# A decode step of attention and MLP: accumulator rows as products of 512 columns, and the other 64 columns of up to eight rows in one product

## The chip, the cores and the metric

The kernel runs on one core of one Trainium2 chip. The metric is the time of one execution on the device, in microseconds; the number given for a kernel is the median of several executions. A profile of one execution stands beside it.

## The reference, cut to what matters

The kernel computes one step of decoding for two sequences: attention against a cache of 4096 keys and values with 32 heads, a two-layer MLP with GELU, and a gate that mixes both. All data are float32.

```python
B, Sq, D = 2, 1, 576;  H, Sk, Dh = 32, 4096, 128;  F = 4608
x = A_x
g = sigmoid((x * gate_w).sum(-1, keepdims=True))
# attention over the cache
q = (x @ wq).reshape(B, Sq, H, Dh).transpose(0, 2, 1, 3)
p = softmax(einsum("bhqd,bhkd->bhqk", q, k_cache) * Dh ** -0.5, axis=-1)
o = einsum("bhqk,bhkd->bhqd", p, v_cache)
a = o.transpose(0, 2, 1, 3).reshape(B, Sq, H * Dh) @ wo        # wo: 4096 x 576
# MLP
b = gelu(x @ w1 + b1, approximate=True) @ w2 + b2              # w2: 4608 x 576
return g * a + (1 - g) * b
```

## The kernel before, in words

**Tiles.** The caches are read in 16 steps (`N`), each with the keys or values of four heads of one sequence (8 MB). In SBUF there is one large tile, `ring`, of three slots; each K, each V and, at the end, each of three groups of rows of w2 and wo (`LAST`) takes the next slot. At the start wq and w1 lie in the same tile, and what is needed for a short time only (`temp`) lies behind them in the third slot. `load()` issues the next transfer of the list `seq` on the queue of SyncE (SP); `load_next` says that a slot's content is used up and issues what may now go there. The last group goes into the slot of the last V.

**A step.** VectorE (DVE) multiplies the K tile by q (L483), GpSimd (POOL) and DVE add up along the head's dimension (L487 to L489), DVE takes the maximum (L493), TensorE (PE) spreads it (L498), ScalarE (ACT) takes the exponential (L508), and TensorE multiplies V by the weights (`av`, L519): 32 products of 512 columns. A product has 32 columns of weights at most, and four of them go to the four groups of 32 output partitions in turn. `keep` (L531) and `combine` (L537) put the step's result into `oall`.

**The output rows.** The second half of the MLP and the output projection are sums of products of one row each: row r of w2 (36 rows, of 128 partitions each), the part `wx` (the last row of w2, split up), and row r of wo (32 rows). Each row has 576 columns. `acc_mm` (L355) adds such a row into the accumulator `acc` in PSUM: two products of 288 columns with two columns of weights each (for the two sequences), at partitions 64 * (r % 2) + 32 * s for the halves s. So `acc` holds four partial sums of 288 columns. It starts with b2 times 1 - g. `mlp_out` does rows of w2, `mlp_x` the part `wx`, `wo_out` rows of wo.

**The order at the end** is written by hand: behind the last scores `mlp_out(0, 24)`, then the last V's `av`, `keep` and `combine`, then `norm_sum`, `norm_t` and `o_turn` (the scaled result of the attention is transposed into `oP`), with further rows of w2 between them, then `mlp_x` and `wo_out(0, FOLD)` with FOLD = 23. `last_out` copies `acc` to SBUF (L438), multiplies wo's rows 23 to 31 into `res` (L441: four products of 144 columns a row, at four groups of partitions), adds the four partial sums of `acc` by products with `fold` behind row 26 (L452), copies `res` and writes the output (L464). wo's rows arrive in pieces, the last ones in pieces of one row and less, so that each is multiplied as it lands.

**At the start** there are products of x with wq and w1 (L291), a first accumulating product of b2 (L355 with g1z), the GELU on DVE and ACT, which gives `hg`, and `hx` for the part `wx` (L397 to L407).

Of the kernel before, what the change touches and what calls it, by code (L numbers as in the profile page):

```python
# [8 lines left out]
F32 = mybir.dt.float32  # L9
AF = mybir.ActivationFunctionType  # L10
ALU = mybir.AluOpType
AX = mybir.AxisListType
P = 128
# [6 lines left out]
def kernel(  # L20
# [14 lines left out]
    nc = tc.nc  # L35
    B, H, SK, DH = k_cache.shape
    D = x.shape[-1]
# [21 lines left out]
    NC = 4  # L59
    DO = D // NC  # L60
    NS = 2
    DS = D // NS
    SCALE = float(DH) ** -0.5
    SLOTS = 3

    LAST = (
        (("w2", 0, 14), ("w2", 14, 28)),
        (("w2", 28, 35), ("wx", 0, 4), ("wo", 0, 9), ("wo", 9, 17)),
        (("wo", 17, 23), ("wo", 23, 27), ("wo", 27, 30), ("wo", 30, 31), ("wo", 31, 32)),
    )  # L70
    FOLD = 23
    SLOT = R * DH
# [8 lines left out]
    cp = ctx.enter_context(tc.tile_pool(name="cp", bufs=1))  # L81
# [4 lines left out]
    ps_acc = ctx.enter_context(tc.tile_pool(name="ps_acc", bufs=1, space=bass.MemoryType.PSUM))  # L86
    ps_av = ctx.enter_context(tc.tile_pool(name="ps_av", bufs=2, space=bass.MemoryType.PSUM))
    ps_big = ctx.enter_context(tc.tile_pool(name="ps_big", bufs=1, space=bass.MemoryType.PSUM))
    ps_o = ctx.enter_context(tc.tile_pool(name="ps_o", bufs=1, space=bass.MemoryType.PSUM))
# [6 lines left out]


    ring = rp.tile([P, SLOTS * SLOT], F32, name="ring")
    kt, vt, wqt, w1t, rows = {}, {}, {}, {}, {}
    seq = [(w, c) for w in ("wq", "w1") for c in range(len(ROWS[w]) + 1)]  # L100
    for i in range(N):
        seq += [("k", i), ("v", i)]
# [19 lines left out]
    def slot(n):  # L122
        k = len(held) % SLOTS
        return ring[:, k * SLOT:k * SLOT + n]
# [8 lines left out]
    NR = NF - 1  # L133
# [3 lines left out]
    def load_last(m):  # L137
        n = sum(z - a for _, a, z in LAST[m]) * D

        used["e"], used["z"] = len(held) % SLOTS * SLOT + n, (len(held) % SLOTS + 1) * SLOT  # L140
        t = slot(n)
        o = 0
        for w, a, z in LAST[m]:
            if w == "wx":
                x2 = t[:32, o:o + z * D]
                rows[w] = x2
                o += z * D
                for c in range(4):
                    nc.sync.dma_start(x2[c::4].rearrange("e (s n) -> e s n", s=4), srcx2[c])
                continue  # L150

            ends = (a * D, a * D + DS, a * D + DS + DO, z * D) if (w, z) == ("wo", 32) else (a * D, z * D)
            for u, v in zip(ends, ends[1:]):
                nc.sync.dma_start(t[:, o:o + v - u], srcs[w][:, u:v])
                o += v - u
            for r in range(a, z):
                rows[w, r] = t[:, o - (z - r) * D:o - (z - r - 1) * D]

    def temp(n, parts=P):
        t = ring[:parts, used["t"]:used["t"] + n]  # L160
        used["t"] += n
        assert used["t"] <= SLOTS * SLOT
        return t

    def late(n, parts=P):
        t = ring[:parts, used["e"]:used["e"] + n]
        used["e"] += n
        assert not seq and used["e"] <= used["z"]
# [28 lines left out]
    b2r = temp(D, 1)  # L197
# [17 lines left out]
    ident = cp.tile([P, P], F32, name="ident")  # L215
# [3 lines left out]
    idsc = cp.tile([P, P], F32, name="idsc")  # L219
    nc.vector.tensor_scalar_mul(idsc, ident, SCALE)  # L220

# [4 lines left out]
    NO = N * E  # L226
    pt = []
    for j in range(NPB):
        t = cp.tile([P, NT * EB + 32 - EB], F32, name=f"p{j}")
# [39 lines left out]
    g1 = cp.tile([P, B], F32, name="g1")  # L269
# [76 lines left out]

    acc = ps_acc.tile([P, DS], F32, name="acc")

    def acc_mm(lhsT, rhs, k, start=False, stop=False):
        m = lhsT.shape[-1]
        for s in range(NS):
            o = 64 * (k % 2) + 32 * s
            nc.tensor.matmul(  # L355
                acc[o:o + m], lhsT, rhs[:, s * DS:(s + 1) * DS], start=start, stop=stop, skip_group_check=True
            )

    g1z = cp.tile([1, 2, 32], F32, name="g1z")
    nc.vector.memset(g1z, 0.0)  # L360
    nc.vector.tensor_copy(g1z[:, 0, :B], g1[0:1])
    for k in range(2):
        acc_mm(g1z[:, k], b2r, k, start=True)

    fold = cp.tile([P, NS, B], F32, name="fold")
    nc.vector.tensor_add(
        fold, ident[:, :P // 2].rearrange("p (s c) -> p s c", s=NS)[:, :, :B],
        ident[:, P // 2:].rearrange("p (s c) -> p s c", s=NS)[:, :, :B],
    )


    hps = [ps_av.tile([P, 512], F32, tag="av", name=f"hps{m}") for m in range(FB - 1)]
# [12 lines left out]
    hg = cp.tile([P, NF, B], F32, name="hg")  # L385
    t = temp(NF * B).rearrange("p (r b) -> p r b", b=B)
# [4 lines left out]
    nc.vector.tensor_scalar(t, t, 1.0, 0.5, op0=ALU.add, op1=ALU.mult)  # L391
    nc.vector.tensor_mul(t, t, hb)
    nc.vector.tensor_mul(hg, t, g1.unsqueeze(1).to_broadcast([P, NF, B]))
    load()

    mod4 = cp.tile([P, 4], F32, name="mod4")
    nc.vector.tensor_reduce(mod4, ident.rearrange("p (q s) -> p s q", s=4), AX.X, ALU.add)  # L397
    div4 = cp.tile([P, 32], F32, name="div4")
    nc.vector.tensor_reduce(div4, ident.rearrange("p (q s) -> p q s", s=4), AX.X, ALU.add)
    hm = cp.tile([P, 4, B], F32, name="hm")  # L400
    nc.vector.tensor_mul(
        hm, hg[:, NR:].to_broadcast([P, 4, B]), mod4.unsqueeze(2).to_broadcast([P, 4, B])
    )
# [2 lines left out]
    hx = cp.tile([32, 4, B], F32, name="hx")  # L406
    nc.vector.tensor_copy(hx.rearrange("p s b -> p (s b)"), hxps)  # L407

    def mlp_x():
        for s in range(4):  # L410
            acc_mm(hx[:, s], rows["wx"][:, s * D:(s + 1) * D], s)

    def mlp_out(lo, hi):
        for r in range(lo, hi):
            acc_mm(hg[:, r], rows["w2", r], r)

    KB = DH // 32
    oP = cp.tile([P, B, 32], F32, name="oP")  # L420

    def o_turn(turn):
        t = late(B * 32).rearrange("p (b c) -> p b c", c=32)
        for b in range(B):
            nc.vector.transpose(t[:, b], oT[:, b])
        ps = ps_sm.tile([P, B * 32], F32, tag="sm", name="op_t")
        nc.tensor.matmul(ps, turn, t.rearrange("p b c -> p (b c)"), start=True, stop=True)
        nc.vector.tensor_copy(oP.rearrange("p b c -> p (b c)"), ps)

    def wo_out(lo, hi):  # L430
        for r in range(lo, hi):
            acc_mm(oP[:, :, r], rows["wo", r], r)


    def last_out():
        res = ps_big.tile([32 * (NC - 1) + B, DO], F32, tag="big", name="res")
        sums = late(DS)
        nc.scalar.copy(sums, acc)  # L438

        def part(r, s):  # L440
            nc.tensor.matmul(  # L441
                res[32 * s:32 * s + B], oP[:, :, r], rows["wo", r][:, s * DO:(s + 1) * DO],
                start=r == FOLD, stop=r == 31, skip_group_check=True,
            )

        for r in range(FOLD, 31):
            for s in range(NC):
                part(r, s)
            if r == FOLD + 3:
                for s in range(NC):  # L450
                    h, o = divmod(s * DO, DS)
                    nc.tensor.matmul(  # L452
                        res[32 * s:32 * s + B], fold[:, h], sums[:, o:o + DO],
                        start=False, stop=False, skip_group_check=True,
                    )

        osb = late(D, B)
        for h in ((0, 1), (2,), (3,)):
            for s in h:
                part(31, s)  # L460
            for s in h:
                cpy = nc.vector.tensor_copy if s % 2 == 0 else nc.scalar.copy
                cpy(osb[:, s * DO:(s + 1) * DO], res[32 * s:32 * s + B])  # L463
        nc.sync.dma_start(out.rearrange("b s d -> (b s) d"), osb)  # L464
# [2 lines left out]
    st, mx, mt, bias, avs = {}, {}, {}, {}, {}  # L467
    oT = cp.tile([P, B, H], F32, name="oT")

    oall = ps_o.tile([NO, 512], F32, name="oall")  # L470
    gall = cp.tile([NO, 1], F32, name="gall")
    gsel = cp.tile([NO, B], F32, name="gsel")
    nc.vector.tensor_reduce(
# [30 lines left out]
    def softmax(i):  # L504
        p = pt[i % NPB][:, :NT * EB].rearrange("p (t c) -> p t c", c=EB)
        for e in range(E):
            w = slice(e * PE_, (e + 1) * PE_)
            nc.scalar.activation(  # L508
                p[w, :, e * RB:(e + 1) * RB], st[i][w].rearrange("p (t c) -> p t c", c=RB), AF.Exp,
                bias=bias[i][w, e:e + 1], scale=SCALE, accum_out=rs[w, i * E + e:i * E + e + 1],  # L510
            )
# [47 lines left out]
    for i in range(N):  # L559
        k = i - 1  # L560
# [18 lines left out]
    k = N - 1  # L579
    max_n(k)  # L580
    softmax(k)
    mlp_out(0, 24)
    av(k)
    load_next(("v", k))
    assert not seq
# [3 lines left out]
    nc.vector.tensor_copy(turn.rearrange("p (h k) -> p k h", k=KB), ident.rearrange("p (k h) -> p k h", k=KB))  # L589
    osum = late(DH, NO)  # L590
    norm_sum()
    mlp_out(24, 30)
    norm_t()
    mlp_out(30, 33)
    o_turn(turn)
    mlp_out(33, NR)
    mlp_x()
    wo_out(0, FOLD)
    last_out()
# [28 lines left out]
```

## Time and profile before

| | |
|---|---|
| median of 3 runs | 723.1 us (721.8 to 723.15) |
| the profiled execution | 723.16 us |
| its span, first to last instruction | 721.0 us |
| busy: DVE, PE, POOL, ACT | 518.4, 237.9, 143.2, 37.8 us |
| DMA queue of SP | 308.55 MB, 99.0% of 16 engines |
| mean rate | 428 GB/s over the span |

A product of float32 shows as two MATMUL records in the profile, so xcounts of TensorE are twice the number of products in the code. In a row of the timeline stand the start, the length, engine and line, the operation, and what ended the idle time before it. PEld are the weight loads of TensorE. The granted clock is the share of TensorE's full clock.

### The profile page before, as it was taken

The numbers are of one execution on the slowest core, as the hardware profiler recorded it, in microseconds if no ns is written. First come the engines' busy times: TensorE is split into PE (matmuls) and PEld (weight loads), VectorE is DVE, ScalarE is ACT, GpSimd is POOL, SyncE is SP. The second block draws the span as 40 slices with busy tenths as digits, with TensorE's granted clock in tenths as the row PEclk, the third lists the DMA queues.
The fourth block names the chain that finished last, engine by engine and source line by source line (L and its number), as shares of the span: only waits on it lengthen the run. The fifth ranks groups of instructions, "written<-read, shape, count | busy, mean of one in ns | idle before, by whom it ended". The sixth has DMA issues, their size and how long they took to land.

```text
span 721.0 us, 3934 instructions
## 1 busy us (share of the span) xinstructions
PE 237.9 (33%) x1675; PEld 72.7 (10%) x1675; DVE 518.4 (72%) x154; ACT 37.8 (5%) x141; POOL 143.2 (20%) x28
## 2 busy tenths in 40 slices
PE   0754022240416060604142230506060603123197
PEld 0321000010101010101010000101010101000032
DVE  0004969889696969696969789696969596978810
ACT  0010010100001010101010100001010101010000
POOL 1000130404050404021130404040504012040400
PEclk9977557575757575655757575757575665757599
DMA  9999999999999999999999999999999999999996
GB/s 408 411 449 423 436 436 419 451 419 451 422 451 423 444 429 440 419 436 429 437 433 433 440 434 433 440 429 444 425 440 425 426 436 433 436 436 434 418 429 277
DMA packets 7261, 308.84 MB, mean 428 GB/s; under 512 B 830, under 2 KB 1214, under 8 KB 1612
## 3 DMA queue, kind: packets, MB, share of 16 engines
q1 hardware_dynamic: 7220, 308.55, 99.0%
q8 instruction: 13, 0.21, 0.1%
q10 hardware_dynamic: 24, 0.05, 0.0%
q14 instruction: 4, 0.03, 0.0%
HBM read 308.59 MB, written 0.00 MB: 428 GB/s over the span
## 4 chain that ended last, share of the span: by engine, by line
DMA 46%; DVE 35%; PE 17%; ACT 1%; issue 1%; POOL 0%; ACTq 0%; DVEq 0%; SPq 0%; POOLq 0%
DMA ring<-in_A_k_cache_dram 39%; DVE ring L483 19%; DVE s L488 10%; PE av L519 9%; DVE s L489 5%; DMA ring<-in_A_wo_dram 3%; DMA ring<-in_gate_w_dram 3%; PE hps L291 2%; PE qps L291 1%; PE oall L537 1%; PE acc L355 1%; PE mt L498 1%; DMA ring<-in_B_b_dram 1%; ACT p L508 1%; PE qps L316 0%
## 5 line engine op out<-in xcount | busy, mean ns | idle before, releaser
L483 DVE TENSOR_TENSOR ring<-ring,q 128x16384 f32<-128x16384 f32 x16 | 275.6, 17225 | 103.7 <-DMA ring<-in_A_k_cache_dram 103.7
L487 POOL TENSOR_TENSOR ring<-ring 128x3968 f32<-128x3968 f32 x16 | 137.0, 8564 | 488.7 <-DVE ring L483 488.7
L488 DVE TENSOR_REDUCE s<-ring 128x66 f32<-128x8448 f32 x16 | 143.3, 8953 | 1.3
L519 PE MATMUL av<-ring,p 128*32 128x512 f32 x1024 | 136.8, 694 | 11.4 <-ACT p L508 6.1
L498 PE MATMUL mt<-idsc,m 128*128 128x128 f32 x32 | 12.7, 500 | 359.8 <-DVE m L493 359.8
L489 DVE TENSOR_REDUCE s<-ring 128x62 f32<-128x3968 f32 x16 | 68.4, 4276 | 0.0
L508 ACT ACTIVATE p<-s,bs 32x128 f32<-32x128 f32 x64 | 25.5, 398 | 485.4 <-DVE bs L502 484.2
L519 PEld LDWEIGHTS av<-ring,p 128*32 128x32 f32 x1024 | 36.1, 126 | 121.8 <-issue 105.1
L498 PEld LDWEIGHTS mt<-idsc,m 128*128 128x128 f32 x32 | 8.0, 313 | 375.5 <-DVE m L493 314.2
L537 PE MATMUL oall<-avs,pick 128*64 128x512 f32 x32 | 30.6, 1059 | 0.8 <-DVE avs L531 0.8
L339 PE MATMUL qb<-qm,spread 64*128 64x512 f32 x8 | 7.3, 1014 | 70.4 <-POOL qm L335 70.4
L531 DVE TENSOR_TENSOR avs<-av,selr 128x512 f32<-128x512 f32 x16 | 10.9, 682 | 16.3 <-PE av L519 16.3
L249 DVE COPY ring<-ring 3x64 f32<-3x64 f32 x2 | 0.3, 182 | 19.1 <-DMA ring<-in_gate_w_dram 19.1
L378 DVE TENSOR_TENSOR ring<-hps,ring 128x384 f32<-128x384 f32 x3 | 1.7, 559 | 15.9 <-PE hps L291 15.7
L335 POOL TENSOR_TENSOR qm<-qall,mine 64x512 f32<-64x512 f32 x4 | 4.1, 1032 | 44.7 <-ACT qall L318 44.7
L310 DVE COPY ring<-ident 128x8 f32<-128x8 f32 x8 | 0.7, 169 | 15.5 <-DMA ring<-in_B_b_dram 15.5
L508 ACT ACTIVATION_READ_ACCUMULATOR p<-s,bs 32x1 f32 x64 | 11.8, 184 | 0.0
L291 PE MATMUL hps<-ring 128*32 128x384 f32 x120 | 11.5, 549 | 0.0
L355 PE MATMUL acc<-ring,hg 128*2 128x288 f32 x140 | 11.3, 467 | 0.0
L291 PE MATMUL qps<-ring 128*32 128x512 f32 x80 | 10.2, 668 | 0.0
L463 DVE COPY ring<-res 2x144 f32<-2x144 f32 x2 | 0.6, 300 | 13.1 <-PE res L441 13.0
L339 PEld LDWEIGHTS qb<-qm,spread 64*128 64x128 f32 x8 | 1.8, 279 | 73.4 <-POOL qm L335 73.4
(88 smaller groups left out, 76.3 us busy)
## 6 DMA issues: line engine op xcount, KB each, us to landing
ring<-in_B_w_dram SPq DMA_DIRECT2D x2, 4608.0 KB
ring<-in_B_w_dram SPq DMA_DIRECT2D x2, 4032.0 KB
ring<-in_A_wo_dram SPq DMA_DIRECT2D x1, 2592.0 KB
ring<-in_A_wo_dram SPq DMA_DIRECT2D x1, 2304.0 KB
ring<-in_B_w_dram SPq DMA_DIRECT2D x1, 2016.0 KB, 12.7
ring<-in_A_wo_dram SPq DMA_DIRECT2D x1, 1728.0 KB
ring<-in_B_w_dram SPq DMA_DIRECT2D x1, 1152.0 KB
ring<-in_A_wo_dram SPq DMA_DIRECT2D x1, 1152.0 KB, 19.0
```

The lines of the kernel that those rows point to most:

```text
L291: nc.tensor.matmul(ps[32 * j:32 * j + 32, :width], lhs, ts[c][:, o:o + width], start=(k == 0), stop=last, skip_group_check=True,)
L339: nc.tensor.matmul(ps, spread, t.rearrange("p u d -> p (u d)"), start=True, stop=True)
L355: nc.tensor.matmul(acc[o:o + m], lhsT, rhs[:, s * DS:(s + 1) * DS], start=start, stop=stop, skip_group_check=True)
L483: nc.vector.tensor_mul(kt[i], kt[i], qs[i].unsqueeze(1).to_broadcast([P, R, DH]))
L487: nc.gpsimd.tensor_add(t[:, :, :DH2], t[:, :, :DH2], t[:, :, DH2:])
L488: nc.vector.tensor_reduce(st[i][:, HALVED:], kt[i][:, HALVED:], AX.X, ALU.add)
L489: nc.vector.tensor_reduce(st[i][:, :HALVED], t[:, :, :DH2], AX.X, ALU.add)
L498: nc.tensor.matmul(mt[i], mx[i].to_broadcast([P, P]), idsc, start=True, stop=True)
L508: nc.scalar.activation(p[w, :, e * RB:(e + 1) * RB], st[i][w].rearrange("p (t c) -> p t c", c=RB), AF.Exp, bias=bias[i][w, e:e + 1], scale ...
L519: nc.tensor.matmul(ps[32 * j:32 * j + 32], p[:, EB * t:EB * t + 32], vt[i][:, RB * t:RB * (t + 1)].rearrange("p r d -> p (r d)"), start=(t ...
L531: nc.vector.tensor_mul(t, avs[i].rearrange("p (r d) -> p r d", d=DH), selr.unsqueeze(2).to_broadcast([P, RB, DH]))
L537: nc.tensor.matmul(oall, pick[:, NO - E - i * E:2 * NO - E - i * E], avs[i].rearrange("p r d -> p (r d)"), start=(i == 0), stop=(i == N - ...
```

## The change

- `acc` gets 512 columns. A row's first 512 columns are one product, at partitions 32 * (r % 4). So `acc` holds four partial sums of 512 columns.
- The other 64 columns of up to eight neighbouring rows are one product (`rest_mm`): its weights are the two columns of each of the rows (up to 16), its moving operand the last 64 columns of each (up to 512), and it goes to a second accumulator, `part_r`, at partitions from 0 on. Of its result only the blocks on the diagonal are wanted. These products stand behind rows 7, 13, 21, 27 and 34 of w2, behind the part `wx`, and behind rows 7, 15 and 22 of wo.
- `last_out` takes the blocks of the diagonal out of `part_r` on DVE (a multiplication by `ownr` and a sum over the blocks) and adds them with one product with `foldr`, behind the products with `fold`.
- Ahead of the last V's `av` stand rows 0 to 13 of w2 in place of 0 to 23; the others stand behind it.
- Row 16 of wo moves from the second group of `LAST` to the third, and the pieces end at rows 8 and 16.
- `res` moves to the PSUM bank of `oall`; `part_r` has the one that `res` had. Some small tiles move from the pool of constants into the third slot, and one `load()` therefore stands behind `hx`.

```diff
+    DM = 512
+    DR = D - DM
+    NB = DM // DR
...
-        (("w2", 28, 35), ("wx", 0, 4), ("wo", 0, 9), ("wo", 9, 17)),
-        (("wo", 17, 23), ("wo", 23, 27), ("wo", 27, 30), ("wo", 30, 31), ("wo", 31, 32)),
+        (("w2", 28, 35), ("wx", 0, 4), ("wo", 0, 8), ("wo", 8, 16)),
+        (("wo", 16, 23), ("wo", 23, 27), ("wo", 27, 30), ("wo", 30, 31), ("wo", 31, 32)),
...
-    acc = ps_acc.tile([P, DS], F32, name="acc")
-
-    def acc_mm(lhsT, rhs, k, start=False, stop=False):
+    acc = ps_acc.tile([P, DM], F32, name="acc")
+
+    def acc_mm(lhsT, rhs, k, start=False):
         m = lhsT.shape[-1]
-        for s in range(NS):
-            o = 64 * (k % 2) + 32 * s
-            nc.tensor.matmul(
-                acc[o:o + m], lhsT, rhs[:, s * DS:(s + 1) * DS], start=start, stop=stop, skip_group_check=True
-            )
+        o = 32 * (k % 4)
+        nc.tensor.matmul(acc[o:o + m], lhsT, rhs[:, :DM], start=start, stop=False, skip_group_check=True)
...
-    for k in range(2):
-        acc_mm(g1z[:, k], b2r, k, start=True)
+    for k in range(4):
+        acc_mm(g1z[:, min(k, 1)], b2r, k, start=True)
+    b2t = cp.tile([1, DR], F32, name="b2t")
+    nc.vector.tensor_copy(b2t, b2r[:, DM:])
...
+    def rest_mm(lhsT, rhs, n):
+        start = not part_r
+        if start:
+            part_r.append(ps_big.tile([NB * B, DM], F32, tag="big", name="acc_r"))
+            assert n == NB
+        nc.tensor.matmul(
+            part_r[0][:n * B, :n * DR], lhsT, rhs[:, :, DM:], start=start, stop=False, skip_group_check=True
+        )
+        if start:
+            nc.tensor.matmul(
+                part_r[0][:B, :DR], g1[0:1], b2t, start=False, stop=False, skip_group_check=True
+            )
...
     def mlp_out(lo, hi):
         for r in range(lo, hi):
             acc_mm(hg[:, r], rows["w2", r], r)
+            for a, z in ((0, 8), (8, 14), (14, 22), (22, 28), (28, 35)):
+                if r == z - 1:
+                    g = a - a % 14
+                    rest_mm(
+                        hg[:, a:z].rearrange("p r b -> p (r b)"), runs["w2", g][:, a - g:z - g], z - a
+                    )
...
     def wo_out(lo, hi):
         for r in range(lo, hi):
-            acc_mm(oP[:, :, r], rows["wo", r], r)
+            acc_mm(oP[:, r], rows["wo", r], r)
+            for a, z in ((0, 8), (8, 16), (16, FOLD)):
+                if r == z - 1:
+                    rest_mm(oP[:, a:z].rearrange("p r b -> p (r b)"), runs["wo", a], z - a)
...
     def last_out():
-        res = ps_big.tile([32 * (NC - 1) + B, DO], F32, tag="big", name="res")
-        sums = late(DS)
+        res = ps_o.tile([32 * (NC - 1) + B, DO], F32, tag="o", name="res")
+        sums = late(DM)
         nc.scalar.copy(sums, acc)
+        own = late(DM, NB * B).rearrange("p (r n) -> p r n", n=DR)
+        nc.vector.tensor_mul(
+            own, part_r[0].rearrange("p (r n) -> p r n", n=DR), ownr.unsqueeze(2).to_broadcast([NB * B, NB, DR])
+        )
+        tail = late(DR, NB * B)
+        nc.vector.tensor_reduce(tail, own.rearrange("p r n -> p n r"), AX.X, ALU.add)
...
-                    h, o = divmod(s * DO, DS)
+                    n = min(DO, DM - s * DO)
                     nc.tensor.matmul(
-                        res[32 * s:32 * s + B], fold[:, h], sums[:, o:o + DO],
+                        res[32 * s:32 * s + B, :n], fold, sums[:, s * DO:s * DO + n],
                         start=False, stop=False, skip_group_check=True,
                     )
+                nc.tensor.matmul(
+                    res[32 * s:32 * s + B, n:], foldr, tail, start=False, stop=False, skip_group_check=True,
+                )
...
-    mlp_out(0, 24)
+    mlp_out(0, 14)
     av(k)
...
-    mlp_out(24, 30)
+    mlp_out(14, 20)
     norm_t()
-    mlp_out(30, 33)
+    mlp_out(20, 24)
     o_turn(turn)
-    mlp_out(33, NR)
+    mlp_out(24, NR)
     mlp_x()
     wo_out(0, FOLD)
     last_out()
```

More of the change, by code (lines that the diff above doesn't have):

```diff
@@ L98 @@
     ring = rp.tile([P, SLOTS * SLOT], F32, name="ring")
-    kt, vt, wqt, w1t, rows = {}, {}, {}, {}, {}
+    kt, vt, wqt, w1t, rows, runs = {}, {}, {}, {}, {}, {}
     seq = [(w, c) for w in ("wq", "w1") for c in range(len(ROWS[w]) + 1)]
@@ L145, in load_last @@
                 x2 = t[:32, o:o + z * D]
-                rows[w] = x2
+                runs[w, 0] = x2.rearrange("p (r n) -> p r n", n=D)
                 o += z * D
@@ L155, in load_last @@
                 o += v - u
+            runs[w, a] = t[:, o - (z - a) * D:o].rearrange("p (r n) -> p r n", n=D)
             for r in range(a, z):
@@ L345 @@
     q_unit(0)
-    acc = ps_acc.tile([P, DS], F32, name="acc")
-    def acc_mm(lhsT, rhs, k, start=False, stop=False):
+    acc = ps_acc.tile([P, DM], F32, name="acc")
+    def acc_mm(lhsT, rhs, k, start=False):
         m = lhsT.shape[-1]
-        for s in range(NS):
-            o = 64 * (k % 2) + 32 * s
-            nc.tensor.matmul(
-                acc[o:o + m], lhsT, rhs[:, s * DS:(s + 1) * DS], start=start, stop=stop, skip_group_check=True
-            )
-    g1z = cp.tile([1, 2, 32], F32, name="g1z")
+        o = 32 * (k % 4)
+        nc.tensor.matmul(acc[o:o + m], lhsT, rhs[:, :DM], start=start, stop=False, skip_group_check=True)
+    g1z = temp(64, 1).rearrange("p (k c) -> p k c", k=2)
     nc.vector.memset(g1z, 0.0)
     nc.vector.tensor_copy(g1z[:, 0, :B], g1[0:1])
-    for k in range(2):
-        acc_mm(g1z[:, k], b2r, k, start=True)
[L365 to L368, printed above, removed]
-    )
+    for k in range(4):
+        acc_mm(g1z[:, min(k, 1)], b2r, k, start=True)
+    b2t = cp.tile([1, DR], F32, name="b2t")
+    nc.vector.tensor_copy(b2t, b2r[:, DM:])
+    fold = cp.tile([P, B], F32, name="fold")
+    nc.vector.tensor_reduce(
+        fold, ident.rearrange("p (g c) -> p c g", g=4)[:, :B], AX.X, ALU.add
+    )
+    foldr = cp.tile([NB * B, B], F32, name="foldr")
+    nc.vector.tensor_reduce(
+        foldr, ident[:NB * B, :NB * B].rearrange("p (r b) -> p b r", b=B), AX.X, ALU.add
+    )
+    ownr = cp.tile([NB * B, NB], F32, name="ownr")
+    nc.vector.tensor_reduce(
+        ownr, ident[:NB * B, :NB * B].rearrange("p (r b) -> p r b", b=B), AX.X, ALU.add
+    )
+    part_r = []
+    def rest_mm(lhsT, rhs, n):
[10 more added lines that the diff above has]
+            )
     hps = [ps_av.tile([P, 512], F32, tag="av", name=f"hps{m}") for m in range(FB - 1)]
@@ L393 @@
     nc.vector.tensor_mul(hg, t, g1.unsqueeze(1).to_broadcast([P, NF, B]))
-    load()
-    mod4 = cp.tile([P, 4], F32, name="mod4")
+    mod4 = temp(4)
     nc.vector.tensor_reduce(mod4, ident.rearrange("p (q s) -> p s q", s=4), AX.X, ALU.add)
-    div4 = cp.tile([P, 32], F32, name="div4")
+    div4 = temp(32)
     nc.vector.tensor_reduce(div4, ident.rearrange("p (q s) -> p q s", s=4), AX.X, ALU.add)
-    hm = cp.tile([P, 4, B], F32, name="hm")
+    hm = temp(4 * B).rearrange("p (s b) -> p s b", b=B)
     nc.vector.tensor_mul(
@@ L407 @@
     nc.vector.tensor_copy(hx.rearrange("p s b -> p (s b)"), hxps)
+    load()
     def mlp_x():
         for s in range(4):
-            acc_mm(hx[:, s], rows["wx"][:, s * D:(s + 1) * D], s)
+            acc_mm(hx[:, s], runs["wx", 0][:, s], s)
+        rest_mm(hx.rearrange("p s b -> p (s b)"), runs["wx", 0], 4)
     def mlp_out(lo, hi):
@@ L415, in mlp_out @@
             acc_mm(hg[:, r], rows["w2", r], r)
+            for a, z in ((0, 8), (8, 14), (14, 22), (22, 28), (28, 35)):
[4 more added lines that the diff above has]
+                    )
     KB = DH // 32
-    oP = cp.tile([P, B, 32], F32, name="oP")
+    oP = cp.tile([P, 32, B], F32, name="oP")
     def o_turn(turn):
@@ L427, in o_turn @@
         nc.tensor.matmul(ps, turn, t.rearrange("p b c -> p (b c)"), start=True, stop=True)
-        nc.vector.tensor_copy(oP.rearrange("p b c -> p (b c)"), ps)
+        nc.vector.tensor_copy(oP, ps.rearrange("p (b c) -> p c b", b=B))
     def wo_out(lo, hi):
         for r in range(lo, hi):
-            acc_mm(oP[:, :, r], rows["wo", r], r)
+            acc_mm(oP[:, r], rows["wo", r], r)
+            for a, z in ((0, 8), (8, 16), (16, FOLD)):
+                if r == z - 1:
+                    rest_mm(oP[:, a:z].rearrange("p r b -> p (r b)"), runs["wo", a], z - a)
     def last_out():
-        res = ps_big.tile([32 * (NC - 1) + B, DO], F32, tag="big", name="res")
-        sums = late(DS)
+        res = ps_o.tile([32 * (NC - 1) + B, DO], F32, tag="o", name="res")
+        sums = late(DM)
         nc.scalar.copy(sums, acc)
+        own = late(DM, NB * B).rearrange("p (r n) -> p r n", n=DR)
+        nc.vector.tensor_mul(
+            own, part_r[0].rearrange("p (r n) -> p r n", n=DR), ownr.unsqueeze(2).to_broadcast([NB * B, NB, DR])
+        )
+        tail = late(DR, NB * B)
+        nc.vector.tensor_reduce(tail, own.rearrange("p r n -> p n r"), AX.X, ALU.add)
         def part(r, s):
             nc.tensor.matmul(
-                res[32 * s:32 * s + B], oP[:, :, r], rows["wo", r][:, s * DO:(s + 1) * DO],
+                res[32 * s:32 * s + B], oP[:, r], rows["wo", r][:, s * DO:(s + 1) * DO],
                 start=r == FOLD, stop=r == 31, skip_group_check=True,
@@ L450, in last_out @@
                 for s in range(NC):
-                    h, o = divmod(s * DO, DS)
+                    n = min(DO, DM - s * DO)
                     nc.tensor.matmul(
-                        res[32 * s:32 * s + B], fold[:, h], sums[:, o:o + DO],
+                        res[32 * s:32 * s + B, :n], fold, sums[:, s * DO:s * DO + n],
                         start=False, stop=False, skip_group_check=True,
                     )
+                nc.tensor.matmul(
+                    res[32 * s:32 * s + B, n:], foldr, tail, start=False, stop=False, skip_group_check=True,
+                )
         osb = late(D, B)
@@ L468 @@
     oT = cp.tile([P, B, H], F32, name="oT")
-    oall = ps_o.tile([NO, 512], F32, name="oall")
+    oall = ps_o.tile([NO, 512], F32, tag="o", name="oall")
     gall = cp.tile([NO, 1], F32, name="gall")
```

## The prediction

> **What bounds the kernel now.** I read the page first (span and the two DMA rows), then the chain of waits for the last 80 us, then the timeline of TensorE alone for the last 40 us, then the busy time by stretch.
>
> ```profile
> span 721.0 us, 3934 instructions
> ...
> DMA  9999999999999999999999999999999999999996
> ```
>
> The 16 DMA engines are over 90% busy in every slice but the last. Nothing in the first 680 us can be made shorter by other products: what can move is the end, where the last rows of wo land and are multiplied. The chain of waits there (start, length, what):
>
> ```profile
> 692.58 3.49 PE av L519 x32
> 696.07 20.26 DMA ring<-in_A_wo_dram
> ...
> 716.37 1.97 PE res L441 x40
> ...
> 718.36 0.27 ACT ring L463
> ```
>
> The last transfers are issued when the last V's products have freed their slot, land at 716.3 us, and then come the products of wo's last rows and a copy. The timeline of TensorE shows how it meets these landings (start, length, what, idle time before it):
>
> ```profile
> 682.10 0.80 PE L498 MATMUL mt<-idsc,m 128*128 128x128 f32 x2 [26.15 <-DVE m L493]
> ...
> 684.72 7.86 PE L355 MATMUL acc<-ring,hg 128*2 128x288 f32 x96
> 692.41 7.04 PE L519 MATMUL av<-ring,p 128*32 128x512 f32 x64
> ...
> 700.27 1.07 PE L537 MATMUL oall<-avs,pick 128*64 128x512 f32 x2 [0.82 <-DVE avs L531]
> ...
> 702.90 0.27 PE L554 MATMUL oT_t<-ident,ring 64*128 64x64 f32 x1
> 703.10 1.14 PE L355 MATMUL acc<-ring,hg 128*2 128x288 f32 x12
> 704.17 0.43 PE L427 MATMUL op_t<-ring 128*128 128x64 f32 x2
> 704.54 0.67 PE L355 MATMUL acc<-ring,hg 128*2 128x288 f32 x8
> 705.13 1.15 PE L355 MATMUL acc<-ring,hx 32*2 32x288 f32 x16
> 706.21 4.53 PE L355 MATMUL acc<-ring,oP 128*2 128x288 f32 x68
> 711.55 1.64 PE L355 MATMUL acc<-ring,oP 128*2 128x288 f32 x24 [0.80 <-DMA ring<-in_A_wo_dram]
> 714.29 1.17 PE L441 MATMUL res<-ring,oP 128*2 128x144 f32 x32 [1.10 <-DMA ring<-in_A_wo_dram]
> 715.27 0.43 PE L452 MATMUL res<-ring,fold 128*2 128x144 f32 x8
> 716.37 1.95 PE L441 MATMUL res<-ring,oP 128*2 128x144 f32 x40 [0.67 <-DMA ring<-in_A_wo_dram]
> ```
>
> From 684.7 us on TensorE hardly rests, yet it is ahead of the transfers: it waits for wo 0.80, 1.10 and 0.67 us. These 2.6 us are all the slack there is. Whatever makes TensorE later by less is free, and whatever makes it later by more is paid in full. The busy time by stretch (PE, PEld, DVE, ACT, POOL, then granted clock, DMA share, GB/s):
>
> ```profile
> 684.70:688.50 3.80, 3.80 (x33) 1.14 (x36) 0.00 (x0) 0.63 (x4) 0.00 (x0) 0.50 0.96 410
> 688.50:692.40 3.90, 3.90 (x68) 1.55 (x64) 0.00 (x0) 0.00 (x0) 0.00 (x0) 1.00 0.95 404
> 692.40:699.50 7.10, 7.05 (x68) 1.80 (x60) 0.00 (x0) 0.00 (x0) 0.00 (x0) 1.00 1.05 446
> ...
> 713.30:716.40 3.10, 1.44 (x44) 1.00 (x48) 0.00 (x0) 0.35 (x1) 0.00 (x0) 1.00 0.63 235
> 716.40:718.40 2.00, 1.92 (x40) 0.88 (x40) 0.46 (x2) 0.32 (x2) 0.00 (x0) 1.00 0.04 13
> ```
>
> The DMA share stays near 1 through V's products, so the transfers stand in a queue and do not wait for a slot. And the clock is 0.50 for the first 3.8 us of the accumulator rows.
>
> **The unit of cost.** Weight loads come in fours while V is multiplied (the third row is used further below):
>
> ```profile
> 693.27 0.12 PEld L519 LDWEIGHTS av<-ring,p 128*32 128x32 f32 x4 [0.31 <-issue]
> 693.70 0.12 PEld L519 LDWEIGHTS av<-ring,p 128*32 128x32 f32 x4 [0.31 <-issue]
> ...
> 705.13 0.59 PEld L355 LDWEIGHTS acc<-ring,hx 32*2 32x2 f32 x16 [0.49 <-issue]
> ```
>
> av(15) has 32 products, and x64 records: two instructions each. Four stand in the four 32-column quarters of the array and run together, and a round of four takes 0.43 us for 512 columns. One product alone is no cheaper: combine's (L537, x2, 512 columns) takes 1.07 us, two rounds of 0.43 and about 0.2 of loading and draining. So a quarter is occupied for 2 x 0.43 = 0.86 us by a product of 512 columns, 1.68 ns a column, whatever the other quarters do. The sum therefore goes by the columns that the busiest quarter has to take.
>
> Before, a row gave two products of 288 columns, in two quarters: half of 288 x 1.68 = 0.24 us a row. After, a row is one product of 512 in quarter r % 4: a quarter of 0.86 = 0.215 us. That saves 0.03 us a row. But the products of the other 64 columns (`rest_mm`) all write partitions from 0 on, so all stand in quarter 0, which has its share of the rows as well. Such a product covers 8 rows with 512 columns: 0.86 us for 8 rows, 0.107 us a row. Together 0.32 us a row against 0.24.
>
> The Trainium skill ("TensorE: Matmul & The Clock Gate", Measured speedup vs the span model) says that packed products span one product's time and some 4 ns for each further tile. By that rule, which speaks against this change, a rest product by itself costs as much as four rows; the 1.07 us of the lone product beside the 0.43 us rounds bears it out.
>
> **Before the last V.** `mlp_out(0, 14)` in place of (0, 24). Quarter 0 takes rows 0, 4, 8, 12 (2048 columns), the rest of rows 0 to 7 (512) and of 8 to 13 (384): 2944 columns, 4.95 us at full clock. The first rest product is followed by one of g1 with b2's last 64 columns on one row of the array: 0.11 us of columns; the switch of the rows in use shows only as 0.49 us that the weight loads lose around the hx rows, so 0.1 to 0.6, and I take 0.3. Of these 5.25 us the 3.8 us at clock 0.50 do 1.9; the other 3.35 follow at full clock: 684.7 + 3.8 + 3.35 = 691.85. V's products start 0.55 us earlier than at 692.41, not the 10 rows' worth that the moved rows suggest. The combine, the sums and `norm_sum` follow 0.55 us earlier: the rows after them start at 700.8 in place of 701.33.
>
> The Trainium skill (same page, What's actually happening) lets the clock rise after about 3.4 us of sustained work. By that rule it would rise near 685.5 and the sum below would be 1.5 us less. Here the clock rose at 688.5, 6.4 us after the first products of that burst at 682.1, and I keep the trace's. Should it rise a few us earlier or later in the new program, that is up to 1.5 us either way.
>
> **After the last V.** Columns on quarter 0: rows 14 to 19, two rounds, 1024; rows 20 to 23 and the rest of 14 to 21, 1024; rows 24 to 34, 1536, with rests of 384 and 448; the wx part, 512 and a rest of 256; wo 0 to 22, 3072, with rests of 512, 512 and 448. In all 9728 columns, of which 3072 are rests (5.16 us): 16.34 us. The two turns between stay: 0.2 us (702.90 to 703.10) and 0.37 (704.17 to 704.54), and 0.2 for the switch to 32 rows and back. 700.8 + 17.1 = 717.9 us: only then are the rows before FOLD done. wo's rows have all landed by then (716.3), so the three waits for them are gone. Before, this point was 711.55 + 1.64 = 713.2.
>
> **The last part.** `last_out` now has two DVE steps between the last rest product and the product with `foldr`. Nearest rows:
>
> ```profile
> 699.52 0.69 DVE L531 TENSOR_TENSOR avs<-av,selr 128x512 f32<-128x512 f32 x1 [16.30 <-PE av L519]
> ...
> 701.71 0.68 DVE L549 TENSOR_REDUCE ring<-oall 64x128 f32<-64x512 f32 x1
> ...
> 713.25 0.40 ACT L438 COPY ring<-acc 128x288 f32<-128x288 f32 x1 [27.90 <-PE acc L355]
> ```
>
> The first two handle 512 elements a partition, as `own` and `tail` do (fewer partitions; I take no gain for that): 0.69 + 0.68 and 0.3 for the drain and two semaphores, 1.67 us. Beside this lie the rows 23 to 26 and the fold products, 1.17 + 0.43 with overlap, 1.23 us from start to start; ScalarE's copy of acc (0.40 us for 288 columns, some 0.7 for 512) lies beside it too. Then `foldr`'s product, which stands ahead of rows 27 to 31 in the queue: 64 columns and a switch, 0.3. Rows 27 to 30 start at 717.9 + 1.67 + 0.3 = 719.85 in place of 716.37: 3.5 us later. From there on the same products; row 31 had waited for its landing and no longer does, 0.25 us back. Sum: +3.2 us on the profiled execution's 723.16 us (span 721.0 and 2.16 around it), which lies 0.06 over the median 723.1: **726.4 us**.
>
> **Edits at nothing.** Early rows:
>
> ```profile
> 44.73 0.14 DVE L366 TENSOR_TENSOR fold<-ident 128x4 f32<-128x4 f32 x1
> ...
> 49.64 0.69 PE L355 MATMUL acc<-ring,g1z 1*32 1x288 f32 x8
> ...
> 60.58 1.85 DVE L378 TENSOR_TENSOR ring<-hps,ring 128x384 f32<-128x384 f32 x3 [15.70 <-PE hps L291]
> ...
> 66.71 0.33 SPq L130 DMA_DIRECT2D ring<-in_A_k_cache_dram  x1
> ...
> 67.43 0.15 DVE L407 COPY hx<-hxps 32x8 f32<-32x8 f32 x1 [0.37 <-PE hxps L405]
> ...
> 70.34 17.23 DVE L483 TENSOR_TENSOR ring<-ring,q 128x16384 f32<-128x16384 f32 x1 [2.27 <-DMA ring<-in_A_k_cache_dram]
> ```
>
> The four small DVE steps for b2t, fold, foldr and ownr (0.14 to 0.3 us each) fall into DVE's 15.70 us of waiting; uncovered they would cost about 1 us. The start products of acc grow from 288 to 512 columns, at most 0.5 us ahead of hps; that pushes DVE's chain into the 2.27 us it waits before the first K. `load()` behind hx issues the second K about 0.9 us later than 66.71: SP has nothing queued behind it that could go, and the transfer stands behind the whole first V, which stands behind the first K that lands at 70.3. Uncovered: 0.9 us. Row 16 of wo moves from one slot's transfers to the next: the same bytes on the same queue.
>
> **Rivals.** *The rest products hide.* If the array spread them over the idle time of the other quarters, they would cost a quarter: 1.29 us in place of 5.16. The point is then 714.0, foldr is through by 716.0, before rows 27 to 30 have landed, and the time stays 723.2. It decides as soon as a rest product of 512 costs under about 0.3 us. Against it: one output partition range, so one quarter, and the 1.07 us. For it: only that no product of such a shape (16 columns of weights, eight runs of 64) is in the trace. 0.12.
> *V's slot sets the end.* The chain names V's products ahead of the last transfers. If the rests before V were free, V would start about 2.5 us earlier, and if the transfers followed, the end would be 720.6: faster. It needs the queue to run dry; the DMA share of 1.05 during V's products says that it doesn't. 0.05.
> *The eight runs of 64 columns, 2304 bytes apart, are read slowly.* At twice the price the rests add 5 us after V and 1.5 before: 733. No product of the trace reads so. 0.06.
> *The clock rises 3 us earlier*: 724.9. 0.05.
>
> **How the numbers follow.** The forecast's case has 0.72. Its own bounds: the rests at 1.07 us in place of 0.86 for 512 columns, +1.5 or so; the clock, 1.5 either way; the DVE steps at less on 16 partitions, down to -0.7. So 724.2 to 728.6 for this case alone. The range reaches down to the case without loss, 722.9 to 728.6, and leaves out the slow reads and the faster case, 1 in 10, and a little of the forecast's own. About 0.2%, 1.45 us, can be told from no change here. Slower: 0.72 + 0.06 + 0.05, less a little of the forecast's low end, 0.82; same 0.13; faster 0.05.
>
> **What would show it.** In the changed profile: av(15) starts near 691.9, not near 690; around each rest product the other quarters stand idle, and the rows between cost 0.32 us each; TensorE has no wait for wo's landings left after 701; rows 27 to 30 start near 719.9, behind a DVE chain of two steps; the last wo transfer still lands near 716 to 717. It is wrong if TensorE still waits for wo at the end, if rest products take much less than 0.86 us of their quarter, or if DVE's two steps lie beside the landings.

## The result and the profile after

The changed kernel took 725.48 us (median of 6 runs, 725.08 to 726.35) against 721.87 us for the kernel before in the same runs (721.69 to 723.15): a ratio of the means (725.51 and 722.25 us) of 1.0045, 95% interval 1.0032 to 1.0058, or 3.3 us more. The change makes the kernel slower by less than half a percent. The forecast was 726.4 us, 3.2 us more than the execution it was made against. The profiled execution of the changed kernel took 725.08 us, with a span of 723.1.

The chain that ended last, from the end of the rows ahead of FOLD (start, length, what). No transfer of wo stands in it any more:

```profile
714.11 1.72 PE acc L358 x11
715.83 0.13 PE acc_r L389
715.96 0.14 PE res L484 x5
716.09 0.50 PE acc_r L389
716.60 0.02 issue
716.62 0.69 DVE ring L477
717.34 1.02 DVE ring L481
718.36 0.04 issue
718.40 0.27 PE res L499 x2
718.67 1.37 PE res L484 x40
720.04 0.28 DVE ring L509
```

Before, this chain ran from the last V's products through 20.26 us of transfer to row 27. Now it runs on TensorE up to the last rest product, through the two DVE steps, and through foldr's product (L499) to row 27. The timeline of TensorE in the changed kernel (L358 are the rows, L389 the rest products, L565 V, L484 wo's last rows):

```profile
681.80 0.79 PE L544 MATMUL mt<-idsc,m 128*128 128x128 f32 x2 [27.42 <-DVE m L539]
...
684.42 2.49 PE L358 MATMUL acc<-ring,hg 128*2 128x512 f32 x16
686.73 1.02 PE L389 MATMUL acc_r<-ring,hg 128*16 128x512 f32 x2
...
689.61 0.63 PE L565 MATMUL av<-ring,p 128*32 128x512 f32 x3
...
690.06 7.21 PE L565 MATMUL av<-ring,p 128*32 128x512 f32 x61
...
699.17 1.89 PE L358 MATMUL acc<-ring,hg 128*2 128x512 f32 x12
...
710.52 0.59 PE L389 MATMUL acc_r<-ring,oP 128*16 128x512 f32 x1
710.52 0.60 PE L358 MATMUL acc<-ring,oP 128*2 128x512 f32 x3
710.95 0.59 PE L389 MATMUL acc_r<-ring,oP 128*16 128x512 f32 x1
710.95 2.30 PE L358 MATMUL acc<-ring,oP 128*2 128x512 f32 x13
713.09 0.59 PE L389 MATMUL acc_r<-ring,oP 128*16 128x512 f32 x1
...
716.04 0.54 PE L389 MATMUL acc_r<-ring,oP 128*14 128x448 f32 x1
716.42 1.02 PE L484 MATMUL res<-ring,oP 128*2 128x144 f32 x25
...
718.40 0.27 PE L499 MATMUL res<-ring,foldr 16*2 16x64 f32 x2 [0.59 <-DVE ring L481]
718.60 1.41 PE L484 MATMUL res<-ring,oP 128*2 128x144 f32 x40
```

The waits for wo of 0.80, 1.10 and 0.67 us are gone: TensorE is the one that is late. From one rest product of wo to the next (710.52 to 713.09) eight rows take 2.57 us, 0.32 us a row. Rows 27 to 30 start at 718.60, 2.2 us later than before. By stretch (columns as in the prediction):

```profile
684.70:688.50 3.80, 3.80 (x28) 0.72 (x22) 0.00 (x0) 0.35 (x2) 0.00 (x0) 0.87 0.96 410
...
713.30:716.40 3.10, 3.10 (x24) 0.64 (x17) 0.00 (x0) 0.50 (x1) 0.00 (x0) 1.00 0.59 215
716.40:718.40 2.00, 1.41 (x36) 0.84 (x34) 1.69 (x2) 0.09 (x1) 0.00 (x0) 1.00 0.06 20
```

The transfers are through when they were (DMA share 0.59 and 0.06 in the last two stretches, 0.63 and 0.04 before), and PE is busy for the whole of the stretch in which it had waited half the time. In the first stretch the mean clock is 0.87 where it was 0.50.

### The profile page after: what moved, and what is told of

It is laid out like the page before. It is cut to its first block, busy times and chain, and to the rows that moved or that the text cites. A ratio compares the mean times of both kernels' runs of the same rounds, so it can differ in the third digit from the quotient of the medians.

```text
span 723.1 us, 3735 instructions
## 1 busy us (share of the span) xinstructions
PE 238.0 (33%) x1573; PEld 71.1 (10%) x1573; DVE 520.4 (72%) x159; ACT 38.0 (5%) x141; POOL 143.2 (20%) x28
## 4 chain that ended last, share of the span: by engine, by line
DMA 43%; DVE 35%; PE 19%; issue 1%; ACT 1%; POOL 0%; ACTq 0%; DVEq 0%; SPq 0%; POOLq 0%
DMA ring<-in_A_k_cache_dram 39%; DVE ring L529 19%; DVE s L534 10%; PE av L565 9%; DVE s L535 5%; DMA ring<-in_gate_w_dram 3%; PE acc L358 2%; PE hps L295 2%; PE oall L583 1%; PE qps L295 1%; DMA ring<-in_B_b_dram 1%; PE mt L544 1%; PE acc_r L389 1%; ACT p L554 1%; PE qps L320 1%
## 5 line engine op out<-in xcount | busy, mean ns | idle before, releaser
L529 DVE TENSOR_TENSOR ring<-ring,q 128x16384 f32<-128x16384 f32 x16 | 275.6, 17224 | 99.7 <-DMA ring<-in_A_k_cache_dram 99.7
L565 PE MATMUL av<-ring,p 128*32 128x512 f32 x1024 | 131.0, 667 | 11.4 <-ACT p L554 6.1
L565 PEld LDWEIGHTS av<-ring,p 128*32 128x32 f32 x1024 | 35.9, 122 | 115.9 <-issue 98.1
L314 DVE COPY ring<-ident 128x8 f32<-128x8 f32 x8 | 0.7, 169 | 16.5 <-DMA ring<-in_B_b_dram 16.5
L358 PE MATMUL acc<-ring,hg 128*2 128x512 f32 x70 | 10.7, 628 | 0.0
```

The costliest lines, as they stand in the source:

```text
L358: nc.tensor.matmul(acc[o:o + m], lhsT, rhs[:, :DM], start=start, stop=False, skip_group_check=True)
L529: nc.vector.tensor_mul(kt[i], kt[i], qs[i].unsqueeze(1).to_broadcast([P, R, DH]))
L565: nc.tensor.matmul(ps[32 * j:32 * j + 32], p[:, EB * t:EB * t + 32], vt[i][:, RB * t:RB * (t + 1)].rearrange("p r d -> p (r d)"), start=(t ...
```

## The experiments

Theory A is that of the prediction: the rest products all stand in quarter 0, which has its share of the rows too, and make TensorE later than wo's landings. Rival B puts the cost on the two DVE steps and foldr's product, rival C on the rows that moved behind the last V. Ratios are to the kernel before in the same series of runs, of the means, with the 95% interval; the times beside them are medians.

**Rest products in all four quarters.** The DVE steps stay; the output partition changes. The diff is cut: beside this the edit clears the accumulator by a memset on DVE, and the tiles of the two DVE steps and of foldr have 128 partitions in place of 16.

```diff
+    def rest_start():
+        t = ps_big.tile([P, DM], F32, tag="big", name="acc_r")
+        nc.vector.memset(t, 0.0)
+        part_r.append(t)
+    QUARTER = (3, 2, 1, 3, 3, 0, 3, 0, 1)
...
+        o = 32 * QUARTER[len(done)]
...
-            part_r[0][:n * B, :n * DR], lhsT, rhs[:, :, DM:], start=start, stop=False, skip_group_check=True
+            part_r[0][o:o + n * B, :n * DR], lhsT, rhs[:, :, DM:], start=False, stop=False, skip_group_check=True
```

> The changed kernel with its rest products handed round the four quarters (output partitions 0, 32, 64, 96), the accumulator cleared by one DVE memset ahead of the last softmax, and the diagonal blocks taken out of 128 partitions. Theory A (the rest products load quarter 0 alone, which already has its share of the rows): the busiest quarter has 8256 columns behind the last V in place of 9728 and 2048 ahead of it in place of 2944, together some 4 us less, so the rows ahead of FOLD end near 712.5 and the two DVE steps lie beside the landings: time as before the change, 721.9 (ratio 1.000 to 1.001). Rival B (the two DVE steps and the product behind them cost the time): they are all there, 725 (1.004). Rival C (the rows moved behind the last V cost it): 725 (1.004).

Measured: 0.9999 (0.9990 to 1.0007), 722.64 us against 723.0. The timeline of this kernel's last part, all engines:

```profile
713.43 0.91 PE L393 MATMUL acc_r<-ring,oP 128*14 128x448 f32 x2
...
714.56 0.69 DVE L481 TENSOR_TENSOR ring<-acc_r,ownr 128x512 f32<-128x512 f32 x1 [10.55 <-PE acc_r L393]
715.16 0.51 PE L499 MATMUL res<-ring,fold 128*2 128x144 f32 x8
715.29 1.02 DVE L485 TENSOR_REDUCE ring<-ring 128x64 f32<-128x512 f32 x1
716.37 0.22 PE L503 MATMUL res<-ring,foldr 128*2 128x64 f32 x1 [0.69 <-DVE ring L485]
```

The last rest product ends some two microseconds earlier, and the DVE steps are just as long (0.69 and 1.02 us). They now lie in the time in which the kernel before waited for wo. The whole loss is gone with the place of the rest products: what else the edit touches is a memset more and no less work on DVE. So B's steps cost only where TensorE is late already, and C is not needed. The gain is less than the 4 us that I had worked out (the rest products end near 714.3, not 712.5), and enough by little. In this profile no product of the last part waits for a landing; foldr's product still waits 0.69 us for DVE, and comes at 716.37, when row 27 came in the kernel before.

**A second copy of wo's rest products, in quarter 0 or in quarter 2.** Same work, same shapes, another 32 columns of the array. The diff is the one for quarter 0; for quarter 2 the partitions are `64:64 + n * B`:

```diff
+                    dup = ps_sm.tile([P, DM], F32, tag="sm", name=f"dup{a}")
+                    n = z - a
+                    nc.tensor.matmul(
+                        dup[0:0 + n * B, :n * DR], oP[:, a:z].rearrange("p r b -> p (r b)"),
+                        runs["wo", a][:, :, DM:], start=True, stop=True, skip_group_check=True
+                    )
```

> The changed kernel with each of wo's three rest products issued a second time, into an accumulator that nobody reads, in quarter 0 (partitions from 0 on). Theory A: 1472 more columns of 1.68 ns on the busiest quarter, all on the path: +2.5 us on the changed kernel, 728.0 (1.0085). A rival by which a rest product costs its work shared out over the array: +0.6 us, 726.1 (1.006). A rival by which only the DVE steps at the end matter: +0, 725.5 (1.005).

> The same three further products as in the run with quarter 0, but in quarter 2 (partitions from 64 on). Theory A: quarter 2 has only its six rows of wo there, 3072 columns, and with the further 1472 it has 4544, no more than quarter 0 has already: +0 to +0.4 us on the changed kernel, 725.5 to 725.9 (1.005). A rival by which any rest product stops the whole array for its time: +2.5 us, 728.0 (1.0085).

Measured: quarter 0 gives 1.0070 (1.0056 to 1.0084), 727.55 us; quarter 2 gives 1.0048 (1.0034 to 1.0062), 726.16 us, four runs each, and the fastest with quarter 0 (726.95) is slower than the slowest with quarter 2 (726.47). Quarter 2 adds nothing that can be told from the changed kernel's 1.0045, quarter 0 adds 1.8 us by the ratios, and not quite the 2.5 forecast. The reason is in its timeline:

```profile
717.99 0.92 PE L389 MATMUL acc_r<-ring,oP 128*14 128x448 f32 x2
718.75 0.54 PE L472 MATMUL dup<-ring,oP 128*14 128x448 f32 x1
...
720.82 0.27 PE L505 MATMUL res<-ring,foldr 16*2 16x64 f32 x2
721.01 1.41 PE L490 MATMUL res<-ring,oP 128*2 128x144 f32 x40
```

The last copy stands behind the last real rest product, so the DVE steps run beside it, and foldr's product no longer waits for them (no idle time in its row; 0.59 us in the changed kernel). And with quarter 2:

```profile
710.55 0.59 PE L389 MATMUL acc_r<-ring,oP 128*16 128x512 f32 x1
710.55 0.59 PE L358 MATMUL acc<-ring,oP 128*2 128x512 f32 x1
710.56 0.59 PE L472 MATMUL dup<-ring,oP 128*16 128x512 f32 x1
710.57 0.59 PE L358 MATMUL acc<-ring,oP 128*2 128x512 f32 x1
```

A rest product, its copy and two rows start within 0.02 us of each other: the copy takes no time that quarter 0 did not need anyhow. So a rest product is neither shared out nor does it stop the array; it fills its own quarter.

**Without rest products.**

```diff
         start = not part_r
+        if not start:
+            return
```

> The changed kernel without its rest products but the first (the last 64 columns of all but eight rows are left out of the sums). Theory A: 3456 columns less on quarter 0, 5.8 us of which 5.2 behind the last V, so the landings set the end again: 721.9 (1.000). Rival (rows of 512 columns at four groups of partitions are themselves slower than two products of 288): still over 723.

Measured: 0.9995 (0.9986 to 1.0004), 722.77 us. The rows of 512 columns alone do no harm, and no good either:

```profile
711.44 1.89 PE L358 MATMUL acc<-ring,oP 128*2 128x512 f32 x14 [1.85 <-DMA ring<-in_A_wo_dram]
714.28 1.16 PE L486 MATMUL res<-ring,oP 128*2 128x144 f32 x32 [0.94 <-DMA ring<-in_A_wo_dram]
...
716.25 1.95 PE L486 MATMUL res<-ring,oP 128*2 128x144 f32 x40 [0.38 <-DMA ring<-in_A_wo_dram]
```

TensorE waits for wo again, 3.2 us in all where it had waited 2.6 before the change, and the time is the same.

**The moved rows alone**, in the kernel before:

```diff
-    mlp_out(0, 24)
+    mlp_out(0, 14)
...
-    mlp_out(24, 30)
+    mlp_out(14, 20)
...
-    mlp_out(30, 33)
+    mlp_out(20, 24)
...
-    mlp_out(33, NR)
+    mlp_out(24, NR)
```

> The kernel before with the moved rows alone: rows 0 to 13 of w2 ahead of the last V in place of 0 to 23, the others behind it as in the changed kernel; two products of 288 columns a row as before. Theory A: V's products start some 2.4 us earlier, ten rows (2.4 us) come behind them, so the rows ahead of FOLD end where they did and the landings still set the end: 721.9 (1.000). Rival (the release of the last V's slot sets when wo lands): 2.4 us less, 719.5 (0.9965). Rival C (the moved rows make TensorE late): more than 723 (1.002).

Measured: 1.0001 (0.9992 to 1.0009), 722.96 us against 722.93.

```profile
688.55 7.04 PE L519 MATMUL av<-ring,p 128*32 128x512 f32 x64
...
710.25 1.64 PE L355 MATMUL acc<-ring,oP 128*2 128x288 f32 x24 [0.93 <-DMA ring<-in_A_wo_dram]
712.98 1.16 PE L441 MATMUL res<-ring,oP 128*2 128x144 f32 x32 [1.09 <-DMA ring<-in_A_wo_dram]
...
715.04 1.90 PE L441 MATMUL res<-ring,oP 128*2 128x144 f32 x40 [0.65 <-DMA ring<-in_A_wo_dram]
```

V's products start 3.9 us earlier than before, at 688.55, and free their slot as much earlier; the time does not follow. Of the 3.9 us, 2.4 were forecast for the ten rows; about 1.3 come from the clock, which rose 3.8 us after the burst's first product here and 6.4 us after it before. The rival by which the release of V's slot sets the end is out, although the chain of waits names V's products ahead of the last transfer. The transfers behind V stand in a queue, as the prediction read from the DMA share near 1.

**The moved rows put back**, in the changed kernel (the same four lines the other way round):

> The changed kernel with the rows of w2 put back: 0 to 23 ahead of the last V. Theory A: the columns on quarter 0 from the first row on are the same, only on the other side of V's products: 725.5 (1.005), within 0.3 us. Rival C (the moved rows cost the time): back to 722 to 723 (1.000 to 1.0015).

Measured: 1.0038 (1.0024 to 1.0052), 725.67 us, against the changed kernel's 1.0045. Rival C is out from this side too.

**foldr's product out of the way.**

```diff
-            if r == FOLD + 3:
+            if r == 30:
```

> The changed kernel with the products of fold and foldr behind row 30 of wo in place of row 26. Rows 27 to 30 (0.98 us) then run while DVE takes the diagonal out. Prediction's reading (TensorE is late and the DVE chain of 1.7 us stands on the path with 0.6 us of it uncovered): foldr's product stays at 718.4, row 31 follows it at once: 0.9 us less, 724.5 (1.0035). Rival (the rows behind foldr wait for landings anyway): no difference, 725.5.

Measured: 1.0038 (1.0025 to 1.0052), 725.01 us; 0.5 us less than the changed kernel by the medians, where 0.9 was forecast. The intervals overlap, so the times alone do not tell it from no gain. Its profile shows the mechanism: foldr's product (719.30) has no idle time ahead of it, and row 31 follows at 719.50, 2.5 us behind the start of the other rows at 717.01; in the changed kernel row 31 starts about 3.2 us behind (716.42 to 718.60, and 0.98 for four rows). So, by these two profiles, some 0.7 us of the loss are the uncovered end of the DVE steps, as long as TensorE is late; that the rest of it is the rest products themselves follows from the copies in quarter 0.

**The kernel before once more**, for a second profile: 723.06 us, a span of 720.9.

> The kernel before, unchanged, for a second profile. Its times lie in two groups, 721.7 to 721.9 and 723.1, and the profile so far is of the upper. If the landings of wo set them, a profile of 721.8 shows the last landing some 1.3 us earlier against the last K's landing (66.3 us between 651.2 and 717.5 in the profile so far); if TensorE sets them, the landings lie alike and the rows behind them differ.

Its landings lie as in the first profile, so this run alone tells nothing of the lower group. The profile of the moved rows does, by accident: its execution took 721.78 us, and there row 27, behind its landing, starts at 715.04 and not at 716.37, with the same wait of 0.65 us ahead. In that execution the landings came 1.3 us earlier. The moved rows are not what does it: their times lie in both groups like those of the kernel before (721.8 to 721.9 and 722.9 to 723.3), and without rest products V's products start some 2.8 us earlier than before, near 689.7, while row 27 still waits until 716.25. What makes the landings come earlier in some executions stays open.

## Why the prediction was right

**The unit of cost** held. Rows and rest products of quarter 0 behind the last V were put at 17.1 us. From the first row to the moment when the last rest product leaves its quarter to the next product, 699.17 to 716.42, it is 17.25 us. The 0.32 us a row are there to the digit.

**What the other quarters do** was half right. They do stand idle for part of the time, but not around each rest product, as the prediction has it among its signs: at 710.52 the rest product of rows 0 to 7 and three of the next four rows start together, and the fourth, in quarter 0, follows. It makes no difference to the sum, since quarter 0 is the last in any case.

**The clock** was the one term that lay elsewhere in the profiled run. In the changed kernel it rose at 685.7 us (3.9 us after the burst's first product at 681.80, against 6.4 in the profile before). V's products therefore started at 689.61, three of them beside the last rest product ahead of V, and not at 691.85. The prediction had named a start near 690 as a sign against it; what came earlier is the clock, and the rest products are not free: the first took 1.02 us (686.73). The prediction had priced the clock at 0.5 us for each microsecond: 2.8 us earlier, 1.4 us less, 725.0 us, its rival of 0.05; the profiled execution took 725.08. The run with the moved rows put back had its rise later, and its profiled execution took 726.05 us. It shows on the first rows, eight of them each:

```profile
684.88 3.59 PE L358 MATMUL acc<-ring,hg 128*2 128x512 f32 x16
```

3.59 us here, 2.49 us in the changed kernel. Up to row 13 both have the same products, and the clock rose 6.1 us and 3.9 us behind the burst's first. In six of the ten profiles of this case it rose 3.8 to 4.5 us behind it, in four 5.8 to 6.4. The Trainium skill ("TensorE: Matmul & The Clock Gate", What's actually happening) says that the window in which the activity is measured runs freely, so that the step falls earlier or later, by 500 ns either way. These profiles agree that the products alone do not set it, but they lie up to 2.6 us apart, and only the lower ones are near the 3.4 us that the page names. A kernel that waits for landings can hide this; that the clock makes the spread of the changed kernel's times (725.08 to 726.35 us) is not shown, since one of them has a profile.

**The last part** was put at 1.97 us from the last rest product to row 27 and took 2.18 (716.42 to 718.60). The term that was too small is the second DVE step: 1.02 us, where the nearest row had given 0.68; foldr's product took 0.2 us in place of 0.3 and hid a part of it. The first took 0.69 on 16 partitions, as on 128: no gain by fewer partitions, as assumed. The 1.23 us given for rows 23 to 26 and the products with fold are not in their rows (0.98 us from start to start, 1.41 to the end); nothing hangs on them, since the DVE steps take longer.

**The total** is nearer than its terms. Rows 27 to 30 came at 718.60 and not at 719.85: the clock gave 1.4 us, a burst that began 0.3 us earlier the rest, and the two sums above took 0.36 back. Behind that point rows 27 to 31 took 1.41 us in place of 1.95, more than the 0.25 us named, but the four copies of `res`, two of which had run beside the last products of row 31, now all follow the last product, so the output is issued 0.71 us behind it in place of 0.34: a term that the sum does not have. And the 3.2 us that were forecast and the 3.3 that were measured have different bases. The forecast stands on an execution of the upper group (723.16 us), the mean of the kernel before takes in the lower group too; against the upper group alone the changed kernel's median is 2.4 us more. That both numbers nearly agree is in part luck.

**The edits at nothing** cost nothing, but less by the cover that was named. From the early part of the changed kernel:

```profile
52.13 1.93 PE L358 MATMUL acc<-ring 1*32 1x512 f32 x8
53.99 11.65 PE L295 MATMUL hps<-ring 128*32 128x384 f32 x120
...
71.38 0.33 SPq L133 DMA_DIRECT2D ring<-in_A_k_cache_dram  x1
...
71.85 17.21 DVE L529 TENSOR_TENSOR ring<-ring,q 128x16384 f32<-128x16384 f32 x1
```

The start products of acc took 1.93 us in place of 0.69, for which I had allowed 0.5 us more, and hps starts 3.7 us later than before. Most of this is not the change's: the biases had landed 1.4 us later in this run (the copy of L314 starts at 44.70, before at 43.33), and the granted clock from 50.1 to 54.0 us was 0.50, where those products had run at 1.00 and 0.95 before, so the product ahead of them took 2.07 us in place of 1.12 and they themselves had half the clock. DVE's first K starts at 71.85 with no idle time ahead, 1.5 us later than before: the 2.27 us of cover were used up. `load()` stands at 71.38 in place of 66.71, 3.9 us by the later chain and 0.8 by its new place, near the 0.9 forecast. What hid it is the next cover: DVE waits for every later K, 99.7 us in 15 waits, where it had waited 103.7 in 16, and at the end the scores are no later (TensorE's product of the last maximum at 681.80, before 682.10).

**The rivals and the range.** That the rest products hide is refuted by the copies in quarter 0; that V's slot sets the end, by the moved rows alone; that the runs of 64 columns are read slowly, by the rest products themselves: 0.43 us from the first to the second instruction (710.52 to 710.95), as for V's. The upper end of the range was put too low for its own terms: 1.5 us for the rest products and 1.5 for the clock on 726.4 give 729.4, not 728.6.

## What to carry to other kernels

Products that share the array by groups of output partitions are to be counted group by group: the time is that of the fullest group, and a product that is put together from others' remains is dear if it always lands in the same one. Here the same products, dealt out over the four groups, cost nothing. And before TensorE is made faster or slower near the end, look at its waits for the last landings: here less work behind them earned nothing (0.9995), and the 2.6 us of waits were all that more work could hide in.

## What the runs showed of the hardware that was not expected

A product can start ahead of an earlier one that stands in another group of columns: in the run with copies in quarter 2 two rows start at 710.55 and 710.57 beside the rest product and its copy, while the rows that come before them in the order of the code, in the quarters of those two, follow one product later, at 711.41. The profile does not name the rows; which is which follows from the quarters that are taken.

The DVE sum over the blocks (64 sums of 8, read with a step) took 1.02 us for 512 elements a partition, on 16 partitions as on 128; the sum over four of `oall`, read with a step too but from PSUM, took 0.68 for the same number. Which of these differences makes it longer was not tried.
